# Layer-norm halves of token blocks 3 and 4 finished in their PSUM banks, and the steps around them re-timed

## The chip, the cores and the metric

The kernel runs on one core of one Trainium2 chip. The metric is device time in microseconds (us) of one execution; a comparison uses the median of several runs. TensorE (PE) does the matmuls, VectorE (DVE), ScalarE (ACT) and GpSimd (POOL) do the elementwise work, and SyncE (SP) issues most DMA transfers. Each engine takes its own instructions strictly in program order and waits on semaphores for the others.

## The reference

All arrays are float32. There are 2048 tokens of width 576, 32 query heads and 16 key/value heads of width 128, and a gated MLP of width 4608. Only the last 512 cached keys and values are attended to.

```python
mod = (silu(c) @ w_mod).reshape(1, 6, 1, -1)
sa, ca, ga, sb, cb, gb = mod[:, 0], ..., mod[:, 5]
h = layernorm(x) * (1 + ca) + sa
x = x + ga * attention(h)        # q = h @ wq; softmax(q k^T / sqrt(128)) v; @ wo
h = layernorm(x) * (1 + cb) + sb
x = x + gb * mlp(h)              # ((relu(h @ W_gate)) * (h @ W_up)) @ W_down
```

## The kernel before

**Split operands.** Every float32 matmul operand is held as a rounded part ("hi", type fp32r) and the remainder ("lo"), and a product is made of three matmuls: hi·hi, lo·hi and hi·lo. So each tensor that feeds PE costs one rounding copy and one subtraction.

**Blocks and units.** The tokens are four blocks of 512 (`qb` 0 to 3; the title's blocks 3 and 4 are `qb` 2 and 3). The attention is 128 units, one for each head and block. Units 0 and 1 are block 0 for heads 0 and 1, units 2 and 3 are block 1, units 4 and 5 block 2, units 6 and 7 block 3. While unit `u` computes its scores and its softmax, the same stretch of the program projects the query of unit `u+1`, multiplies probabilities and values of unit `u-1`, and makes pieces of the output projection (`wo`) of older units. So block 2 must be normalised before the projection that stands in unit 3 (`qps` of unit 4), and block 3 before the one in unit 5.

**Order.** The main loop calls the parts of a unit in a fixed order. Between them stand hooks `run(u, k)`, k from 0 to 9, which emit all "steps" whose time is at most `10*u + k`. A step is a piece of side work with a number written by hand: `step("a2.tr0", 29, ...)` is emitted in unit 2 at hook 9. The order of the calls is the order on each engine's queue; SP's DMA issues follow it too, each waiting until its buffer is free.

**Layer norm.** `norm_steps` makes the steps for a block: `stats` (DVE: mean and variance of four tiles of 128 tokens), `rstd` (POOL), `norm` (ACT: `xna`), then for the column groups (0,1), (2,3) and (4): `trans` (PE transposes `xna` into a PSUM bank `lta`) and `affine`. `affine` multiplies by the modulation column and adds the other (`lfa`, an SBUF tile, from `lta` in PSUM), rounds `lfa` to the hi part (`hTa_0` to `hTa_3` and `hTa_8`), and subtracts that from `lfa` to get the lo part (`hTa_4` to `hTa_7`, and the upper half of `hTa_8`). A string such as "aav" says which engine does each of the three passes (a: ACT, v: DVE, p: POOL). `trans` takes its bank from one of three PSUM pools, named "s", "w" and "m" in the table of steps: "s" (two buffers, also the scores), "w" (one, also the `wo` pieces and the gate row `mps`) and "mm" (two, also `qps`, `qm` and `pv`).

**Maxima.** The softmax maxima of a unit are spread over partitions by a small PE matmul (`qm`, in PSUM). `max_bc` reduces them to `r`. In the first four units and the last one (`by_pe`) `r` is split into parts (`rh`, `rr`), transposed on DVE (`mb`), copied by ACT (`mr`), and PE subtracts it from the scores by matmuls with `minus`; in the other units DVE subtracts.

**Gate row and first output weights.** `m2.0` to `m2.4` sum up five pieces of the modulation's third row on DVE (`wmb`), `ga` spreads it by PE (`mps`) and ACT (`mrow`), and the first two output weights are loaded (`wo0.l`, `wo1.l`; tile `roga`), multiplied by it on DVE (`.g`), and split by ACT and POOL (`.c`; tile `woga`).

A `wo` piece is added to the residual by DVE (`acc`), or, where no other user of the "w" bank stands between two pieces, ACT copies the residual into the bank first and the sum back after it ("seeded").

## Time and profile before

| | |
|---|---|
| time, three runs | 2917.99 us median (2914.55 to 2919.14) |
| profiled execution | 2925.96 us, its span 2923.5 us |
| PE busy | 2858.1 us, 98% of the span |
| DVE, POOL, ACT busy | 2161.4 (74%), 2117.4 (72%), 1489.4 (51%) us |
| mean granted TensorE clock | 0.993 |

A row of a timeline gives start, duration, engine, source line, operation, output and inputs with buffer numbers left out, how many instructions are merged into it, and in brackets the idle time before it and what ended that. A row of a table by windows gives the stretch and its length, the busy time of each engine with the number of instructions, and then the granted clock, the DMA engines' share and GB/s. A row of waits gives who waited for whom, the total, how often, and the longest.

### The profile page before, as it was taken

Reading aid. Unit: us, or ns where it says so; the run is one execution under the profiler, and the core shown is the slowest. Engines: PE = TensorE matmul, PEld = TensorE weight load, DVE = VectorE, ACT = ScalarE, POOL = GpSimd, SP = SyncE. Lnnn points to the kernel's source line nnn. Section 1 sums busy time; section 2 is a strip of 40 time slices with the busy share of each in tenths; the row PEclk is TensorE's granted clock in tenths of the full one; section 3 lists DMA queues with packets and bytes.
Section 4 is the critical chain, followed back from the end, with each engine's and each line's share of the span. In section 5 each row is a group of like instructions: output and inputs, shape, how many; then the busy total and the mean of one; then the engine's idle time right before and its main releaser. Section 6 shows DMA issues by size and latency. Waiting matters only on the chain. (4 is left out here: it accounts for less than half of the span.)

```text
span 2923.5 us, 41266 instructions
## 1 busy us (share of the span) xinstructions
PE 2858.1 (98%) x15214; PEld 2490.0 (85%) x15214; DVE 2161.4 (74%) x2981; ACT 1489.4 (51%) x2095; POOL 2117.4 (72%) x1564
## 2 busy tenths in 40 slices
PE   6799999999999999999999999999999999999999
PEld 4588888888888888888888888888888888888888
DVE  7888888888888888777889755666676466666666
ACT  4466666666676666666656444444444122222221
POOL 4588888888889889876778666777787356656553
PEclk9899999999999999999999999999999999999999
DMA  4011222222223223322144456666666944444443
GB/s 151 22 45 53 85 91 80 71 101 90 89 89 108 84 69 118 116 70 86 65 129 144 142 210 220 226 230 224 224 222 251 340 160 152 151 152 153 157 151 104
DMA packets 162697, 396.43 MB, mean 136 GB/s; under 512 B 14912, under 2 KB 61760, under 8 KB 162496
## 3 DMA queue, kind: packets, MB, share of 16 engines
q1 hardware_dynamic: 131472, 282.15, 30.2%
q10 hardware_dynamic: 31024, 111.65, 9.7%
q8 instruction: 120, 1.97, 0.3%
q14 instruction: 81, 0.66, 0.1%
HBM read 268.73 MB, written 153.32 MB: 144 GB/s over the span
## 5 line engine op out<-in xcount | busy, mean ns | idle before, releaser
L539 POOL TENSOR_TENSOR lo<-p,hi 128x1024 fp32r<-128x1024 f32 x256 | 610.0, 2405 | 1.1 <-ACT hi L519 1.1
L548 POOL TENSOR_TENSOR ks<-ks,p 128x512 f32<-128x512 f32 x256 | 344.0, 1344 | 271.8 <-ACT p L532 208.7
L460 DVE TRANSPOSE_TENSOR_REDUCE t<-s 128x32 f32<-128x1024 f32 x256 | 316.8, 1244 | 136.4 <-PE s L457 125.0
L943 PE MATMUL gu<-hop_B,wop 128*128 128x512 f32 (+1 forms) x1512 | 379.0, 394 | 0.9 <-DMA wop<-wk_P 0.9
L943 PEld LDWEIGHTS gu<-hop_B,wop 128*128 128x128 f32 (+1 forms) x1512 | 276.3, 188 | 53.6 <-issue 1.3
L383 PE MATMUL qps<-hTa,wA 128*128 128x512 f32 x1288 | 312.4, 394 | 9.7 <-ACT lfa L365 7.7
L943 PE MATMUL gu<-hop_T,wop 128*128 128x512 f32 (+1 forms) x1260 | 319.9, 393 | 0.0
L599 PE MATMUL wo<-woga,ohi 128*128 128x288 f32 x1472 | 305.9, 301 | 1.5 <-DVE lfa L363 1.5
L383 PEld LDWEIGHTS qps<-hTa,wA 128*128 128x128 f32 x1288 | 244.7, 190 | 62.1 <-ACT lfa L365 8.2
L530 DVE TENSOR_TENSOR p<-s,mb 128x1024 f32<-128x1024 f32 x246 | 290.3, 1219 | 4.1
L519 ACT CAST hi<-p 128x1024 fp32r<-128x1024 f32 x256 | 269.1, 1051 | 7.1
L599 PE MATMUL md<-wogb,hhi 128*128 128x288 f32 x1280 | 263.4, 298 | 5.8 <-DVE acc L610 4.9
L532 ACT ACTIVATE p<-p 128x1024 f32<-128x1024 f32 x246 | 259.9, 1056 | 8.0 <-DVE p L530 7.9
L943 PEld LDWEIGHTS gu<-hop_T,wop 128*128 128x128 f32 (+1 forms) x1260 | 228.4, 188 | 41.0
L610 DVE TENSOR_TENSOR acc<-md,acc 128x576 f32<-128x576 f32 x160 | 120.9, 756 | 177.5 <-PE md L599 177.1
L435 ACT ACTIVATE qhi<-qps 128x512 fp32r<-128x512 f32 x128 | 76.5, 598 | 341.1 <-PE qps L383 341.1
L599 PEld LDWEIGHTS wo<-woga,ohi 128*128 128x128 f32 x1472 | 238.7, 188 | 9.1 <-issue 1.9
L599 PEld LDWEIGHTS md<-wogb,hhi 128*128 128x128 f32 x1280 | 214.9, 190 | 19.1 <-DVE acc L610 6.3
L1054 DVE TENSOR_TENSOR acc<-st_P,acc 128x576 f32<-128x576 f32 x160 | 121.1, 757 | 133.7 <-PE st_P L1045 133.7
L599 PE MATMUL wo<-woga,olo 128*128 128x288 f32 x736 | 216.9, 295 | 0.3 <-POOL olo L588 0.2
L599 PE MATMUL md<-wogb,hlo 128*128 128x288 f32 x640 | 190.1, 297 | 0.0
L588 POOL TENSOR_TENSOR olo<-rb,ohi 128x512 fp32r<-128x512 f32 x128 | 167.3, 1307 | 23.6 <-ACT ohi L584 23.1
(269 smaller groups left out, 7106.6 us busy)
## 6 DMA issues: line engine op xcount, KB each, us to landing
wop<-wk_P SPq DMA_DIRECT2D x133, 640.0 KB
wk_P<-wop ACTq DMA_DIRECT2D x119, 640.0 KB
wr<-wlay SPq DMA_DIRECT2D x68, 384.0 KB
rogb<-wd SPq DMA_DIRECT2D x68, 288.0 KB
againq<-akq SPq DMA_DIRECT2D x18, 640.0 KB
rwA<-wq SPq DMA_DIRECT2D x32, 320.0 KB
wlay<-wg SPq DMA_DIRECT2D x36, 256.0 KB
roga<-wo SPq DMA_DIRECT2D x32, 288.0 KB
```

What stands on the lines that cost most here:

```text
L383: return [lambda i=i, a=a, b=b: nc.tensor.matmul(ps, a, b, start=(i == 0), stop=(i == n - 1)) for i, (a, b) in enumerate(ops)]
L460: nc.vector.tensor_reduce(t4[u][:, 2 * h:2 * h + 2, :].rearrange("p k b -> p (k b)"), t.rearrange("p k (b j) -> p (k b) j", j=32), axis=AX ...
L519: nc.scalar.copy(hi_[u, h], pt[u, h])
L530: nc.vector.tensor_tensor(p, t, bc[u][:, None, :].to_broadcast([P, 2, 512]), op=ALU.subtract)
L532: nc.scalar.activation(p, p, AF.Exp, bias=0.0, scale=1.0)
L539: nc.gpsimd.tensor_sub(lo_[u, h], pt[u, h], hi_[u, h].bitcast(F32))
L548: nc.gpsimd.tensor_tensor(ks_[u], ks_[u], p[:, j, :], op=ALU.add)
L588: nc.gpsimd.tensor_sub(olo[u], o.pop(u), ohi[u].bitcast(F32))
L599: nc.tensor.matmul(ps[:, half, :H2], a[:, sl], w[b][:, cs], start=(n == 0 and seed is None), stop=(n == 5), skip_group_check=seed is not None)
L610: nc.vector.tensor_tensor(av, ps[:, :, :H2], av, op=ALU.add)
L943: nc.tensor.matmul(ps, a, c, start=s not in heir(m) and i == 0 and s not in seeds_of(m), stop=i == len(ops) - 1, skip_group_check=True)
L1054: nc.vector.tensor_tensor(t, ps[:, :, :H2], t, op=ALU.add)
```

## The change

1. For blocks 2 and 3 `affine` makes no `lfa`. It writes the hi part straight from the PSUM bank, then writes the full result back into the same bank, and a new step (`.lo`) lets DVE subtract the hi part from the bank. Engines by group: block 2 "aav", "vvv", "aav"; block 3 "aav" three times.
2. The group (0,1) is transposed after the scores of units 3 and 5 (steps 30.5 and 50.5 and a new hook `run(u, .5)`) instead of ahead of them, group (2,3) of block 3 in the "s" pool one hook earlier, and group (4) of it in "mm". The projections of units 4 and 6 take the groups in the order (2,3), (4), (0,1), with the lo parts of 1 and 0 last.
3. In the `by_pe` units `r` lies in the bank of `qm`, and the two parts are made from it there; `rh` and one copy are gone.
4. `m2.2` moves from step 14 to 5, `m2.3` from 14 to 16, the gate row from 19 to 21, the two weights' loads from 19 and 24 to 10 and 11, their multiplications from 20 and 26 to 23, their splits from 24 and 30 to 29 and 32. `rstd` of block 2 moves from 16 to 14, its fourth `xna` tile to another pool, two of block 3's `stats` from 30 to 33.

```diff
@@ LayerNorm.affine
             add, mul = mods[self.key]
+            if qb > 1:
+                out = {d: (h[8], h[8][64:]) if d == 4 else (h[d], h[4 + d]) for d in ds}
+                for n in range(2):
+                    for d, e in zip(ds, engs):
+                        a, m = add[:, d:d + 1], mul[:, d:d + 1]
+                        dst = self.ps[d] if n else out[d][0]
+                        if e[n] == "v":
+                            nc.vector.tensor_scalar(dst, self.ps[d], m, a, op0=ALU.mult, op1=ALU.add)
+                        else:
+                            nc.scalar.activation(dst, self.ps[d], AF.Identity, bias=a, scale=m)
+                def rest():
+                    for d in reversed(ds):
+                        p0 = 64 if d == 4 else 0
+                        nc.vector.tensor_sub(out[d][1], self.ps[d][p0:], out[d][0].bitcast(F32)[p0:])
+                self.rest[ds] = rest
+                return
@@ proj_ops (late: u in (4, 6))
+        if late:
+            his((2, 3)); both(); los((2, 3)); his((0, 1)); los((1, 0))
...
@@ max_bc
-        r = sp.tile([P, 16], F32, tag="r", name=f"r{u}", bufs=1)
+        r = bps[u][:, 256:272] if by_pe(u) else sp.tile([P, 16], F32, tag="r", name=f"r{u}", bufs=1)
...
-            nc.vector.tensor_copy(rh, r)
-            nc.vector.tensor_copy(rr[:, :, 0], rh.bitcast(F32))
-            nc.vector.tensor_sub(rr[:, :, 1], r, rh.bitcast(F32))
+            nc.vector.tensor_copy(rr[:, :, 0], r)
+            nc.vector.tensor_sub(rr[:, :, 1], r, rr[:, :, 0].bitcast(F32))
@@ norm_steps
+            if key == "a" and qb > 1:
+                step(f"{nm}.lo{k}", t_af[k] + (1 if t_af[k] == 45 else 0), lambda ds=ds: ln.rest[ds]())
@@ the table of steps
-    norm_steps("a2", 2, "a", "wC", "raw", (8, 9, 14, 14), 16, (19,) * 4, (29, 26, 29),
-               (29, 26, 29), (("w", "aav", "vvv"), ("w", "vvv", "vvv"), ("m", "aav")))
+    norm_steps("a2", 2, "a", "wC", "wC", (8, 9, 14, 14), 14, (19,) * 4, (30.5, 26, 29),
+               (30.5, 26, 29), (("w", "aav", "aav"), ("w", "vvv", "vvv"), ("m", "aav")))
...
@@ main loop
         s_half(u, 1)
+        run(u, .5)
         max_pre(u)
```

DVE's queue from the end of unit 2 to the scores of unit 3, before (`lfa` is the affine result, `hTa` the hi and lo parts, `rb` the finished output of a unit, `roga` the second output weight):

```order
L363 TENSOR_SCALAR lfa_2_981<-lta_2_968,mcol_454,mcol_499 128x512
L363 TENSOR_SCALAR lfa_3_983<-lta_2_968,mcol_454,mcol_499 128x512
L367 CAST hTa_2_977<-lfa_2_981 128x512
L367 CAST hTa_3_979<-lfa_3_983 128x512
L371 TENSOR_TENSOR hTa_6_978<-lfa_2_981,hTa_2_977 128x512
L371 TENSOR_TENSOR hTa_7_980<-lfa_3_983,hTa_3_979 128x512
L222 TENSOR_TENSOR roga_941<-roga_941,mrow_860 128x576
L580 TENSOR_TENSOR rb_960<-pv_943,rb_960 128x512
L363 TENSOR_SCALAR lfa_1_1018<-lta_0_1003,mcol_454,mcol_499 128x512
L367 CAST hTa_1_1014<-lfa_1_1018 128x512
L371 TENSOR_TENSOR hTa_5_1015<-lfa_1_1018,hTa_1_1014 128x512
L371 TENSOR_TENSOR hTa_4_1013<-lfa_0_1016,hTa_0_1012 128x512
```

The same queue now, from the same place on:

```order
L359 TENSOR_SCALAR hTa_2_966<-lta_2_957,mcol_454,mcol_499 128x512
L359 TENSOR_SCALAR hTa_3_968<-lta_2_957,mcol_454,mcol_499 128x512
L359 TENSOR_SCALAR lta_2_957<-lta_2_957,mcol_454,mcol_499 128x512 x2
L366 TENSOR_TENSOR hTa_7_969<-lta_2_957,hTa_3_968 128x512
L366 TENSOR_TENSOR hTa_6_967<-lta_2_957,hTa_2_966 128x512
L613 TENSOR_TENSOR rb_949<-pv_932,rb_949 128x512
L366 TENSOR_TENSOR hTa_8_994<-lta_4_0_989,hTa_8_994 64x512
L495 TENSOR_REDUCE t_3_1008<-s_0_1001 128x32
L495 TENSOR_REDUCE t_3_1008<-s_1_1010 128x32
L366 TENSOR_TENSOR hTa_5_1030<-lta_0_1018,hTa_1_1029 128x512
L366 TENSOR_TENSOR hTa_4_1028<-lta_0_1018,hTa_0_1027 128x512
```

Each subtraction now has one operand in PSUM, the rounding copies are gone, and the parts of group (0,1) stand behind the score maxima of unit 3 instead of ahead of them.

DVE's queue behind the spread of unit 2's maxima, before (`r` to `rr` are the maxima and their parts):

```order
L498 TENSOR_REDUCE r_923<-qm_903 128x16
L488 RECIPROCAL ri_925<-qm_903 128x16
L505 CAST rh_928<-r_923 128x16
L506 COPY rr_929<-rh_928 128x16
L507 TENSOR_TENSOR rr_929<-r_923,rh_928 128x16
L508 STREAM_TRANSPOSE mb_927<-rr_929 128x512
L493 STREAM_TRANSPOSE rb_960<-ri_925 128x512
L439 SCALAR_TENSOR_TENSOR qlo_962<-qps_907,qhi_936 128x512
```

And now:

```order
L533 TENSOR_REDUCE qm_892<-qm_892 128x16
L523 RECIPROCAL ri_919<-qm_892 128x16
L539 CAST rr_922<-qm_892 128x16
L540 TENSOR_TENSOR rr_922<-qm_892,rr_922 128x16
L541 STREAM_TRANSPOSE mb_921<-rr_922 128x512
L222 TENSOR_TENSOR roga_751<-roga_751,mrow_896 128x576
L222 TENSOR_TENSOR roga_775<-roga_775,mrow_896 128x576
L528 STREAM_TRANSPOSE rb_949<-ri_919 128x512
L474 SCALAR_TENSOR_TENSOR qlo_951<-qps_902,qhi_928 128x512
```

The maxima stay in the bank `qm`, one copy is gone, and both multiplications of output weights by the gate row stand between the transposed maxima and `qlo`, the low part of unit 3's query.

PE's queue at the projection of unit 4 (in unit 3), before; `wA` is the query weight:

```order
L383 MATMUL qps_1068<-hTa_0_1012,wA_471 128x512 x2
L383 MATMUL qps_1068<-hTa_1_1014,wA_471 128x512 x2
L383 MATMUL qps_1068<-hTa_2_977,wA_471 128x512 x2
L383 MATMUL qps_1068<-hTa_3_979,wA_471 128x512 x2
L383 MATMUL qps_1068<-hTa_8_1029,wA_471 128x512 x2
L383 MATMUL qps_1068<-hTa_4_1013,wA_471 128x512
L383 MATMUL qps_1068<-hTa_5_1015,wA_471 128x512
L383 MATMUL qps_1068<-hTa_6_978,wA_471 128x512
L383 MATMUL qps_1068<-hTa_7_980,wA_471 128x512
```

And now:

```order
L418 MATMUL qps_1042<-hTa_2_966,wA_471 128x512 x2
L418 MATMUL qps_1042<-hTa_3_968,wA_471 128x512 x2
L418 MATMUL qps_1042<-hTa_8_994,wA_471 128x512 x2
L418 MATMUL qps_1042<-hTa_6_967,wA_471 128x512
L418 MATMUL qps_1042<-hTa_7_969,wA_471 128x512
L418 MATMUL qps_1042<-hTa_0_1027,wA_471 128x512 x2
L418 MATMUL qps_1042<-hTa_1_1029,wA_471 128x512 x2
L418 MATMUL qps_1042<-hTa_5_1030,wA_471 128x512
L418 MATMUL qps_1042<-hTa_4_1028,wA_471 128x512
```

The eight matmuls that need groups (2,3) and (4) come first; the eight transposes of group (0,1) now stand just ahead of this list, behind the twelve score matmuls of unit 3.

More of the change, by code (lines that the diff above doesn't have):

```diff
@@ L268, in __init__ @@
             self.qb, self.key, self.where = qb, key, where
-            self.xn, self.ps, self.ready, self.n, self.xt = {}, {}, 0, 0, None
+            self.xn, self.ps, self.rest, self.ready, self.n, self.xt = {}, {}, {}, 0, 0, None
         def stats(self, i):
@@ L371, in affine, with proj_ops, his, los @@
                 eng.tensor_sub(out[d][1], fs[d][p0:], out[d][0].bitcast(F32)[p0:])
-    def proj_ops(ps, w, h):
+    def proj_ops(ps, w, h, late=False):
         ops = []
-        for t in range(4):
-            ops.append((w[:, t, :], h[t]))
-            ops.append((w[:, 5 + t, :], h[t]))
-        ops.append((w[:, 4, :], h[8]))
-        ops.append((w[:, 9, :], h[8]))
-        for t in range(4):
-            ops.append((w[:, t, :], h[4 + t]))
+        def his(ts):
+            for t in ts:
+                ops.append((w[:, t, :], h[t]))
+                ops.append((w[:, 5 + t, :], h[t]))
+        def los(ts):
+            for t in ts:
+                ops.append((w[:, t, :], h[4 + t]))
+        def both():
+            ops.append((w[:, 4, :], h[8]))
+            ops.append((w[:, 9, :], h[8]))
+        if late:
+            his((2, 3))
+            both()
+            los((2, 3))
+            his((0, 1))
+            los((1, 0))
+        else:
+            his(range(4))
+            both()
+            los(range(4))
         n = len(ops)
@@ L1296 @@
     for t in range(5):
[L1297 to L1299 removed]
+        step(f"m2.{t}", (4, 4, 5, 16, 16)[t], lambda t=t: mod_step(2, t, big[2, t]))
+    w_use.add(21)
+    step("ga", 21, setd(mods, "ga", lambda: gate_row(2)))
     sss = (("s", "aap", "vvv"), ("s", "aap", "vvv"), ("s", "aav"))
     www = (("w", "aap", "vvp"), ("w", "aap", "vvp"), ("w", "aap"))
[L1302 to L1305 removed]
+    norm_steps("a2", 2, "a", "wC", "wC", (8, 9, 14, 14), 14, (19,) * 4, (30.5, 26, 29),
+               (30.5, 26, 29), (("w", "aav", "aav"), ("w", "vvv", "vvv"), ("m", "aav")))
+    norm_steps("a3", 3, "a", "wC", "raw", (33, 33, 34, 34), 34, (36,) * 4, (50.5, 45, 49),
+               (50.5, 45, 49), (("w", "aav", "aav"), ("s", "aav", "aav"), ("m", "aav")))
     H = 10 * UNITS.index((HKV - 1, 1, HQ - 1))
@@ L1313 @@
     po = prep_out(wos, 0, wo, "ga")
-    step("wo0.l", 19, po[0])
-    step("wo0.g", 20, po[1])
-    step("wo0.c", 24, po[2])
+    step("wo0.l", 10, po[0])
+    step("wo0.g", 23, po[1])
+    step("wo0.c", 29, po[2])
     po = prep_out(wos, 1, wo, "ga")
-    step("wo1.l", 24, po[0])
-    step("wo1.g", 26, po[1])
-    step("wo1.c", 30, po[2])
+    step("wo1.l", 11, po[0])
+    step("wo1.g", 23, po[1])
+    step("wo1.c", 32, po[2])
     def sk(t, key, d, k):
```

12 lines of the change are left out of this document (3 added, 9 removed).

## The prediction

> **What bounds the kernel now.** I read the page's busy shares first (PE 98%), then the engines' times in two stretches, then PE's waits, then the timelines around the longest of them.
>
> ```profile
> 44.00:146.54 102.54, 74.89 (x322) 59.68 (x323) 85.75 (x137) 49.10 (x68) 53.18 (x37) 0.85 0.07 20
> 150.00:500.00 350.00, 350.00 (x1861) 305.38 (x1860) 285.59 (x424) 238.03 (x319) 290.94 (x175) 1.00 0.22 71
> ```
>
> The second figure of a row is its length, the third PE's busy time. From 150 to 500 us PE never idles: the attention is bound by PE, and whatever shifts its queue ahead of 150 us shifts everything behind. The change's instructions stand almost all in units 0 to 5 (44 to 146.54 us), where PE idles 27.65 us of 102.54 and is granted 0.85 of its clock. So the most there is to win is those waits and the slow clock. They are (waits of PE over the whole program):
>
> ```profile
> PE qps L383 <- ACT lfa L365: 7.7, 1, 7.7
> PE lta L323 <- DVE rb L580: 5.6, 1, 5.6
> PE s L526 <- ACT mr L511: 6.2, 4, 3.0
> PE mps L150 <- DVE wmb L129: 2.9, 1, 2.9
> PE wo L599 <- DVE lfa L363: 1.5, 1, 1.5
> ```
>
> The longest is the projection of unit 4 waiting for block 2's norm. There DVE does this, with POOL beside it:
>
> ```profile
> 81.76 1.52 DVE L363 TENSOR_SCALAR lfa<-lta,mcol,mcol 128x512 f32<-128x512 f32 x2
> 82.80 2.70 POOL L548 TENSOR_TENSOR ks<-ks,p 128x512 f32<-128x512 f32 x2 [1.51 <-ACT p L528]
> 83.20 2.58 DVE L367 CAST hTa<-lfa 128x512 fp32r<-128x512 f32 x2
> 85.45 5.32 POOL L539 TENSOR_TENSOR lo<-p,hi 128x1024 fp32r<-128x1024 f32 x2
> 85.70 5.63 DVE L371 TENSOR_TENSOR hTa<-lfa,hTa 128x512 fp32r<-128x512 f32 x2
> 93.81 1.29 DVE L371 TENSOR_TENSOR hTa<-lfa,hTa 128x512 fp32r<-128x512 f32 x2
> 94.60 0.78 ACT L365 ACTIVATE lfa<-lta,mcol,mcol 128x512 f32<-128x512 f32 x1 [4.50 <-DVE hTa L371]
> ```
>
> Two subtractions take 1.29 us with POOL idle and 5.63 us beside POOL. Whether that goes with the operands' place is told by all instances (minimum, median, maximum, ns):
>
> ```profile
> L371 DVE TENSOR_TENSOR hTa<-lfa,hTa x13: 684/691/2878, 28.6 to 136.0; 128x512 fp32r<-128x512 f32 x10, 64x512 fp32r<-64x512 f32 x3
> L505 DVE CAST rh<-r x5: 127/931/1298, 44.8 to 1630.8; 128x16 fp32r<-128x16 f32 x5
> L507 DVE TENSOR_TENSOR rr<-r,rh x5: 169/169/1266, 45.8 to 1632.2; 128x16 f32<-128x16 f32 x5
> L222 DVE TENSOR_TENSOR roga<-roga,mrow x32: 744/750/2368, 69.4 to 1181.5; 128x576 f32<-128x576 f32 x32
> L580 DVE TENSOR_TENSOR rb<-pv,rb x128: 636/680/693, 66.3 to 1657.4; 128x512 f32<-128x512 f32 x128
> L439 DVE SCALAR_TENSOR_TENSOR qlo<-qps,qhi x128: 650/653/692, 35.5 to 1622.1; 128x512 fp32r<-128x512 f32 x128
> ```
>
> The first four read SBUF alone and stretch to several times their least. The last two have one operand in PSUM, and of 256 none passes 0.693 us. The new subtractions (L366, L540) are of the second kind. The Trainium skill ("SBUF — State Buffer", Who interferes with whom) says why: GpSimd shares a port pair with VectorE, held for a whole instruction, and two SBUF inputs or a two-port mode need it. These rows agree.
>
> **The sum.** PE's queue, at the points I count between (brackets: idle before):
>
> ```profile
> 66.46 2.20 PE L150 MATMUL mps<-wmb,ones 128*128 128x288 f32 x4 [2.88 <-DVE wmb L129]
> 68.04 1.04 PE L455 MATMUL s<-qhi,kv 128*128 128x512 f32 x1
> 71.94 3.35 PE L383 MATMUL qps<-hTa,wA 128*128 128x512 f32 x14
> 83.42 1.50 PE L323 MATMUL lta<-ident,xna 128*128 128x128 f32 x12 [1.20 <-DVE lfa L363]
> 84.68 0.47 PE L455 MATMUL s<-qhi,kv 128*128 128x512 f32 x1
> 95.43 5.92 PE L383 MATMUL qps<-hTa,wA 128*128 128x512 f32 x14 [7.75 <-ACT lfa L365]
> 102.42 0.45 PE L483 MATMUL qm<-t,quad 128*128 128x80 f32 x2 [1.07 <-DVE t L475]
> 110.35 0.39 PE L455 MATMUL s<-qhi,kv 128*128 128x512 f32 x1
> 113.10 3.34 PE L383 MATMUL qps<-hTa,wA 128*128 128x512 f32 x14
> 131.25 1.97 PE L323 MATMUL lta<-ident,xna 128*128 128x128 f32 x8 [5.59 <-DVE rb L580]
> 132.87 0.78 PE L455 MATMUL s<-qhi,kv 128*128 128x512 f32 x1
> 140.30 0.45 PE L483 MATMUL qm<-t,quad 128*128 128x80 f32 x2 [0.32 <-DVE t L475]
> 146.54 0.39 PE L455 MATMUL s<-qhi,kv 128*128 128x512 f32 x1
> ```
>
> At full clock 12 score matmuls take 2.75 us (110.35 to 113.10), so 0.23 each; 12 transposes 1.26 (83.42 to 84.68), so 0.84 for 8.
>
> *Maxima, units 0 to 2.* PE waits for `mr` behind `r`. The stalls of one CAST in unit 0 (0.931−0.127 = 0.8) and of a CAST and a subtraction in units 1 and 2 (up to 1.266−0.169 = 1.1 each) go: −3.0. A PSUM result may cost each step 0.1 more; the dropped copy pays that. The bank of `qm` is freed later, and `pv` takes it next; but behind half of `pv` PE waits for `mr` anyway, so nothing.
>
> *Gate row.* The 2.88 us wait goes, because the row is spread behind unit 2's scores; its matmuls and those scores ran slowly (66.46 to 68.04, 68.04 to 71.94 against 2.75), so 0.8 and 1.15 more: −4.8. The multiplications it feeds read SBUF alone and now stand, both, ahead of `qlo` of unit 3, while POOL works: 2×0.75 plus a stall; of that PE sees about +0.5. Earlier weight loads and the later split cost nothing: `woga` is first read by a `wo` piece in unit 3. The cover is half a unit; without it that piece waits. `rstd` on POOL passes ahead of `ks`, which waits for the second exponential anyway. On SP the two loads now pass three layout copies (`wlay`), which nothing reads before the MLP, and wait only for buffers that are free in unit 0; on POOL the weights' low parts stand behind unit 2's `lo`, ahead of nothing that PE is near.
>
> *Unit 2's end.* The wait of 1.20 goes and 8 transposes move behind the scores: −2.0.
>
> *Unit 3 to its spread (84.68 to 102.42: 17.7 us).* Two more rows carry this stretch and unit 5's:
>
> ```profile
> 101.22 0.27 DVE L468 TENSOR_REDUCE qm<-t 128x16 f32<-128x64 f32 x1
> 118.92 1.06 ACT L532 ACTIVATE p<-p 128x1024 f32<-128x1024 f32 x1
> ```
>
> Counted from the first score matmul: `qlo` is ready just ahead, at −0.3. DVE goes on with `ks` (some 0.7), two passes that write hi and two that write the bank (0.76 each, from 81.76) and two subtractions (1.29), and ends at 4.6. PE is done with the scores at 2.75; its next work, eight transposes, needs the "w" bank that DVE still reads: it waits 1.85, transposes (0.84), ends at 5.4. Then eight matmuls run to 7.3 without a wait, four more for `hTa_0` and `hTa_1`. ACT meanwhile makes two hi passes and two into the bank (0.78 the last, 0.72 apart: 3.0), so DVE subtracts from 8.5 to 9.8, PE's last two matmuls wait for that some 1.4 in all, and DVE's `t` (101.22 to 102.42: 1.2) ends at 11.0. In all 11.0 for 17.7: −6.7. The 7.75 us wait and the half clock of the 5.92 us projection are in that.
>
> *Spread to unit 4's scores (102.42 to 110.35: 7.9 us).* The same PE work stands here, and the maxima of unit 3 had no stall to lose. Before, a slow stretch of 3.4 us lay in it; I expect one again, since PE has just worked little (the clock, below). Two more tiles' statistics stand between `mb` and `qlo`, whose third score matmul waits a little: +0.5. Without a slow stretch it is 1.0 less: −0.5.
>
> *Unit 4 (110.35 to 132.87).* The waits of 1.5 and 5.59 go, and eight half-speed transposes (131.25 to 132.87) move behind the scores: −8.7. ACT takes over DVE's add of one `wo` piece, hidden by the next PE work.
>
> *Unit 5 (132.87 to 140.30: 7.4 us).* Here part of it is paid back. Ahead of unit 5's scores PE has 5.6 us of work behind the second `wo` piece (12 `pv` at 0.23, 12 `wo` of 288 columns at 0.13, 12 transposes at 0.105), and ACT in that time two copies (0.63), the first exponential and its rounding (1.06 each), some 3.7 with the hand-overs: so its four passes of group (2,3) start 1.9 before the scores and end 1.1 after they began. The second exponential, which stood there, queues behind them; its readers on POOL are not needed before the next unit. DVE's two subtractions free the score bank at 2.5, where PE, six matmuls in (1.4), has waited 1.1. Scores end at 3.9, transposes at 4.7. ACT comes to `hTa_8` behind the second exponential, its rounding and a copy (2.7) and makes two passes (1.5): done at 5.3, subtracted at 6.0, and PE waits 0.3. A weight's copy (0.7) and four passes (3.0) later, at 9.0, DVE subtracts to 10.2, and `t` ends at 11.4. In all 11.4 for 7.4: +4.0.
>
> *To 146.54.* Same work, but behind a low stretch: +1.5 for a slow window.
>
> Sum: −3.0 −4.8 +0.5 −2.0 −6.7 +0.5 −8.7 +4.0 +1.5 = −18.7. A matmul's end, 0.39 behind its start where the next one follows after 0.23, is counted as work but stood ahead of each lost wait as well: 0.16, some eight times, −1.3. Together −20.
>
> **Unknown price.** No row shows a pass that reads and writes PSUM. Below stands a copy into PSUM, above a read and a write one after the other:
>
> ```profile
> 114.38 0.63 ACT L632 COPY wo<-acc 128x576 f32<-128x576 f32 x1
> ```
>
> So 0.63 to 0.78+0.63 = 1.4 us. I take 0.78, the row of the same operation from PSUM. Nine such passes stand on the chains of units 3 and 5 (two of DVE, seven of ACT): at 1.4 they add 9×0.62 = 5.6 us, at 0.63 they save 1.4.
>
> **The clock.** Stretches of 3.41 us:
>
> ```profile
> 76.82:80.23 3.41, 2.28 (x12) 1.00 0.00 0
> 80.23:83.64 3.41, 2.21 (x14) 1.00 0.31 89
> ...
> 100.72:104.13 3.41, 1.77 (x8) 1.00 0.00 0
> 104.13:107.54 3.41, 3.41 (x10) 0.50 0.00 0
> ```
>
> With 2.28 and 2.21 us of PE work in a stretch the clock stayed; with 1.77, and no idle time over 1.07 in it, the next stretch was slow, which costs up to 1.7 us. Behind both new spreads PE works about 0.8 of 3.9 us, so I count one slow stretch at each. The Trainium skill ("TensorE: Matmul & The Clock Gate", Why this matters for your kernels) warns only of idle gaps above some 3 us between bursts. By that neither place would slow down and the sum would be the first rival's; the 1.77 row speaks against it.
>
> **Rivals.**
> - *No slow stretch.* For it: the longest new wait is 1.85 us, and before the clock mostly fell behind waits of 2.9 us and more. Then the +1.5 goes and the +0.5 becomes −0.5: −22.5, 2895.5. Against: the 1.77 row. Chance 0.13.
> - *Less, by new waits.* In-place passes at 1.4 (+5.6) and two more slow windows (+3.4): −11, 2907. Nearly the same if the subtractions wait for POOL after all, so that the change doesn't do what it says: four that PE waits for, by 2.878−0.684 = 2.2 each, +8.8. Against that: 256 instances. Chance 0.18.
> - *No change.* The front's gain is given back to a DMA later. Against: 350 us of unbroken PE work. Chance 0.07.
> - *Slower.* The many gaps of 0.3 to 1.9 us keep PE at half clock from unit 2 to 5, some 50 us of work at full clock. Each slow stretch costs 1.7 us, so 12 more eat the 20 us; at 50 us of doubled work it would be +30, 2948. Before, with longer gaps, a full stretch always brought the clock back. Chance 0.05.
>
> **The numbers.** Forecast: −20 against the profiled execution's 2925.96 us, and as well against the median, 2917.99, 0.3% lower: 2898. Chance of −14 to −22: 0.57. The range, 2893 to 2909, takes in the first rival's gain (2895.5, and 1.4 more with cheap passes) and the second's loss with 2 us on top; it leaves out the last two rivals (0.12) and the tails of the others. A change of 0.2% (5.8 us) is about what the runs can tell. Faster 0.88, same 0.07, slower 0.05.
>
> **What would show it.** L366 within 0.70 us each, all ten. PE's waits for `lfa`, `rb` and `wmb` gone; new ones for L366 (at the "w" bank 1.9, the score bank 1.2, the last lo parts 1 to 2 twice). Unit 6's scores near 126 us. Clock 0.5 for some 3.4 us behind the spreads of units 3 and 5. I am wrong if L366 stretches beside POOL, if in-place passes exceed 1.4 us, or if the later stages lose what units 1 to 4 won.

## The result, and the profile after

The changed kernel takes 2898.20 us (median of six runs, 2893.46 to 2904.06) against 2918.57 for the kernel before on the same chip (six runs, 2914.55 to 2922.90): a ratio of 0.9932, 95% interval 0.9921 to 0.9942. That is 20.4 us less; the forecast was 2898. Its profiled execution took 2898.73 us, with a span of 2895.9.

First the same stretch by windows as before the change, now from 44 us to the first score matmul of unit 6, and the attention behind it:

```profile
44.00:125.94 81.94, 72.19 (x320) 57.46 (x321) 66.81 (x119) 56.08 (x78) 51.61 (x36) 0.90 0.07 22
150.00:500.00 350.00, 348.48 (x1848) 303.62 (x1848) 286.69 (x424) 235.98 (x317) 291.31 (x174) 1.00 0.22 74
```

Unit 6 starts at 125.94 us instead of 146.54, so the stretch is 20.6 us shorter. Not all of that is the change: unit 0's scores began at 37.05 us in the profiled execution of before and at 35.06 in this one, and in the traces of the experiments below they begin anywhere from 34.2 to 36.9. From unit 0's scores to unit 6's it is 18.6 us. PE's idle time in the stretch fell from 27.65 to 9.75 us, and the granted clock rose from 0.85 to 0.90. Behind it PE is as full as it was: the 1.52 us missing from 350 are one wait, which before stood at 505.70 us, just behind that window.

The rest of the program, from unit 6's scores to the end, is another 7.0 us shorter in these two executions. Of that, 1.1 us are the change: the last unit of the attention makes its maxima in the new way too (x2, below). The other 5.9 lie behind the attention. From unit 6's scores to the end it is 2777.0 us in the kernel before and 2775.9 in x5, which has only the in-place passes, against 2767.7 to 2771.1 in the eleven other kernels, so this may belong to the change too; why is not shown. In the medians, which differ by 20.4, there is little room for it: the profiled execution of before was 7.4 us above its own median.

PE's waits in that stretch of the changed kernel (who waited for whom, total, how often, longest):

```profile
PE pv L605 <- DVE rr L540: 2.8, 3, 0.9
PE s L559 <- ACT mr L544: 2.1, 1, 2.1
PE qps L418 <- DVE hTa L366: 2.1, 4, 0.7
PE lta L323 <- DVE hTa L366: 1.8, 1, 1.8
PE qm L518 <- DVE t L510: 1.1, 2, 0.6
PE s L490 <- DVE hTa L366: 0.8, 1, 0.8
```

The waits of 7.7 for `lfa`, 5.6 for `rb` and 2.9 for `wmb` are gone. New are those for the subtractions, L366: at the "w" bank 1.8, at the score bank 0.8, at the last low parts 0.7 at most. The maxima now hold the bank of `qm` for longer: `pv` waits 2.8 us for it in this stretch, 1.7 before, while the wait for `mr` fell from 5.2 to 2.1. The passes and subtractions themselves (minimum, median, maximum, ns), and one pair of subtractions beside POOL:

```profile
L366 DVE TENSOR_TENSOR hTa<-lta,hTa x10: 680/692/695, 76.6 to 116.4; 128x512 fp32r<-128x512 f32 x8, 64x512 fp32r<-64x512 f32 x2
L361 ACT ACTIVATE lta<-lta,mcol,mcol x8: 738/751/752, 75.0 to 115.0; 128x512 f32<-128x512 f32 x8
76.55 1.29 DVE L366 TENSOR_TENSOR hTa<-lta,hTa 128x512 fp32r<-128x512 f32 x2
76.15 4.68 POOL L572 TENSOR_TENSOR lo<-p,hi 128x1024 fp32r<-128x1024 f32 x2
```

All ten subtractions lie within 0.70 us, though several stand beside POOL, and a pass from a bank into the same bank takes 0.75 us on ACT (0.82 on DVE). PE's queue at the points that the forecast counted between:

```profile
47.05 0.79 PE L490 MATMUL s<-qhi,kv 128*128 128x512 f32 x1 [0.32 <-ACT p L561]
59.77 0.39 PE L490 MATMUL s<-qhi,kv 128*128 128x512 f32 x1
73.24 0.47 PE L490 MATMUL s<-qhi,kv 128*128 128x512 f32 x1
77.99 1.06 PE L323 MATMUL lta<-ident,xna 128*128 128x128 f32 x8 [1.76 <-DVE hTa L366]
84.53 0.58 PE L518 MATMUL qm<-t,quad 128*128 128x80 f32 x2 [0.56 <-DVE t L510]
93.93 0.39 PE L490 MATMUL s<-qhi,kv 128*128 128x512 f32 x1
107.28 0.48 PE L490 MATMUL s<-qhi,kv 128*128 128x512 f32 x1
109.71 0.47 PE L490 MATMUL s<-qhi,kv 128*128 128x512 f32 x1 [0.79 <-DVE hTa L366]
118.15 0.45 PE L518 MATMUL qm<-t,quad 128*128 128x80 f32 x2 [0.55 <-DVE t L510]
125.94 0.39 PE L490 MATMUL s<-qhi,kv 128*128 128x512 f32 x1
```

And the clock around the two spreads, in stretches of 3.41 us (PE's busy time is the third figure, the granted clock the third from the end):

```profile
81.22:84.63 3.41, 2.11 (x8) 0.98 (x6) 2.67 (x6) 1.44 (x3) 2.41 (x2) 1.00 0.00 0
84.63:88.04 3.41, 2.46 (x7) 1.90 (x8) 2.71 (x10) 1.34 (x3) 0.00 (x0) 0.51 0.30 96
88.04:91.46 3.42, 3.42 (x10) 2.65 (x9) 3.25 (x11) 1.80 (x3) 1.66 (x3) 0.50 0.00 0
115.35:118.77 3.42, 2.23 (x10) 1.18 (x9) 2.44 (x6) 0.97 (x2) 2.77 (x2) 1.00 0.00 0
118.77:122.18 3.41, 3.41 (x15) 3.21 (x14) 2.96 (x6) 1.81 (x3) 1.16 (x1) 0.51 0.40 118
```

Slow stretches came behind both spreads, two of them at unit 3's.

### The profile page after: what moved, and what is told of

It reads as the page before. It is cut to its first block, busy times and chain, and to the rows that moved or that the text cites. A ratio compares the mean times of both kernels' runs of the same rounds, so it can differ in the third digit from the quotient of the medians.

```text
span 2895.9 us, 41262 instructions
## 1 busy us (share of the span) xinstructions
PE 2852.8 (99%) x15214; PEld 2485.6 (86%) x15214; DVE 2145.8 (74%) x2967; ACT 1496.0 (52%) x2105; POOL 2115.4 (73%) x1564
## 4 chain that ended last, share of the span: by engine, by line
PE 91%; POOL 3%; DVE 3%; ACT 2%; issue 1%; DMA 1%; SPq 0%; ACTq 0%; POOLq 0%; DVEq 0%
PE gu L976 26%; PE wo L632 13%; PE qps L418 13%; PE md L632 8%; PE st_P L1078 6%; PE s L491 4%; PE s L490 4%; PE s L492 4%; PE pv L607 4%; PE pv L606 4%; PE pv L605 4%; PE qm L518 1%; POOL lo L572 1%; ACT p L565 0%; DVE ws L783 0%
## 5 line engine op out<-in xcount | busy, mean ns | idle before, releaser
L641 ACT COPY acc<-wo 128x576 f32<-128x576 f32 x233 | 148.2, 636 | 66.8 <-PE wo L632 61.6
```

The costliest lines, as they stand in the source:

```text
L641: nc.scalar.copy(av, ps[:, :, :H2])
```

## The experiments

Each run was timed beside the kernel before. Where times differ by a few us, the place is read from the profiled execution. That is one execution, and it lay anywhere from 6.4 us below its kernel's median (x2) to 7.4 above (before), so places and medians need not agree. The table gives the time between the first score matmul of a unit (s) and the spread of its maxima (q), and in the last column how much of s1 to s6 was granted half the clock.

| | median us | s1-s2 | s2-s3 | s3-q3 | q3-s4 | s4-s5 | s5-q5 | q5-s6 | s1-s6 | at half clock |
|---|---|---|---|---|---|---|---|---|---|---|
| before | 2918.57 | 18.19 | 16.64 | 17.74 | 7.93 | 22.52 | 7.43 | 6.24 | 96.69 | 27.0 |
| changed | 2898.20 | 12.72 | 13.47 | 11.29 | 9.40 | 13.35 | 10.87 | 7.79 | 78.89 | 13.8 |
| x1 | 2904.05 | 12.91 | 13.50 | 15.54 | 6.65 | 14.00 | 12.85 | 7.81 | 83.26 | 14.1 |
| x2 | 2904.53 | 13.56 | 15.90 | 10.03 | 7.92 | 13.34 | 10.88 | 6.25 | 77.88 | 6.9 |
| x3 | 2900.52 | 16.98 | 13.24 | 12.26 | 6.65 | 13.99 | 10.89 | 6.24 | 80.25 | 7.8 |
| x4 | 2895.41 | 12.00 | 13.50 | 11.69 | 6.66 | 13.96 | 10.90 | 6.24 | 74.95 | 5.4 |
| x5 | 2914.36 | 17.45 | 20.61 | 10.69 | 9.10 | 21.47 | 6.90 | 6.22 | 92.44 | 24.7 |
| d1 | 2892.13 | 13.08 | 13.47 | 11.29 | 6.75 | 14.01 | 10.88 | 6.23 | 75.71 | 4.3 |
| v2 | 2902.99 | 11.94 | 13.50 | 11.25 | 8.31 | 17.33 | 10.93 | 7.78 | 81.04 | 12.1 |
| best1 | 2898.62 | 11.73 | 13.49 | 11.00 | 6.73 | 18.11 | 11.52 | 6.25 | 78.83 | 8.0 |
| e1 | 2900.25 | 12.83 | 13.49 | 11.28 | 6.75 | 13.99 | 12.53 | 6.22 | 77.09 | 3.8 |
| best2 | 2892.70 | 11.75 | 13.49 | 11.69 | 6.65 | 14.00 | 10.87 | 6.24 | 74.69 | 3.4 |
| best3 | 2891.13 | 11.75 | 13.49 | 10.99 | 6.74 | 14.02 | 10.58 | 6.23 | 73.80 | 0 |

**x1: the second pass writes SBUF.**

```
+                t = pp.tile([P, 1024], F32, tag="p", ...)      # groups (0,1) and (2,3)
+                fs = {d: t[:, 512 * j:512 * j + 512] for j, d in enumerate(ds)}
-                        dst = self.ps[d] if n else out[d][0]
+                        dst = fs[d] if n else out[d][0]
-  nc.vector.tensor_sub(out[d][1], self.ps[d][p0:], ...)
+  nc.vector.tensor_sub(out[d][1], fs[d][p0:], ...)
```

> The changed kernel, but for column groups (0,1) and (2,3) of blocks 2 and 3 the second pass writes an SBUF tile instead of the bank, and the subtraction reads that tile; places, engines and the number of instructions stay. My theory (a DVE instruction with two SBUF inputs is held while POOL works, one with a PSUM operand is not): the pairs of subtractions that stand beside POOL's work stretch from 1.29 us to between 2.5 and 5.6 us, as two of them did before (5.63). Beside POOL stand the pair at 76.55 us, the one at 82.14 and the one at 115.75; the one at 108.28 has POOL idle. The wait of the transposes behind the first pair goes (1.76, the bank is free a pair of subtractions earlier), but the projection of unit 4 waits for it instead. Estimate +2 to +4 for unit 3 and +1 to +2 for unit 5: +3 to +6 us against the changed kernel (2901 to 2904), most of the eight L366 with SBUF operands over 0.9 us. Rival (the new places of the steps make the gain, not the operand's place): all stay within 0.70 us each and the time is that of the changed kernel or up to 2.6 us less, since the banks come free earlier.

Measured: 2904.05 us, ratio to before 0.995 (0.9938 to 0.9962), 5.9 above the changed kernel. DVE's subtractions (L371) and POOL's work beside them:

```profile
76.46 5.52 DVE L371 TENSOR_TENSOR hTa<-lfx,hTa 128x512 fp32r<-128x512 f32 x2
85.75 1.29 DVE L371 TENSOR_TENSOR hTa<-lfx,hTa 128x512 fp32r<-128x512 f32 x2
117.66 3.75 DVE L371 TENSOR_TENSOR hTa<-lfx,hTa 128x512 fp32r<-128x512 f32 x2 [0.22 <-ACT lfx L366]
76.32 5.11 POOL L577 TENSOR_TENSOR lo<-p,hi 128x1024 fp32r<-128x1024 f32 x2
114.19 4.72 POOL L577 TENSOR_TENSOR lo<-p,hi 128x1024 fp32r<-128x1024 f32 x2
118.87 1.98 POOL L182 TENSOR_TENSOR wA<-rwA,wA 128x640 fp32r<-128x640 f32 x1
```

PE's wait for them:

```profile
PE qps L423 <- DVE hTa L371: 9.5, 4, 5.7
```

The first pair starts 0.14 us behind POOL's `lo` instructions and lasts 5.52 us; in the bank the same pair took 1.29. The pair at 117.66 stretches to 3.75. The pair that I had expected to stretch in unit 3's middle had been pushed, by the first one, to where POOL was idle, and took 1.29. PE waits 5.7 us for the first. Unit 3 to its spread is 4.25 longer, but two slow stretches, from 81.61 to 88.43 us, lie in it here and behind the spread in the changed kernel: to unit 4's scores it is 1.5 longer. Unit 5 is 2.0 longer. Only four of the eight subtractions stretched, not most of them. With nothing but the operand's place altered, the time moved as the theory said, and the rival is out. The run says a second thing: with the operand in SBUF, some 15 of the 20 us are still won, by the rest of the change.

**x2: the maxima's parts as before** (r in SBUF, `rh`, one copy more):

```
-        r = bps[u][:, 256:272] if by_pe(u) else sp.tile(...)
+        r = sp.tile([P, 16], F32, tag="r", name=f"r{u}", bufs=1)
+            nc.vector.tensor_copy(rh, r)
+            nc.vector.tensor_copy(rr[:, :, 0], rh.bitcast(F32))
```

> The changed kernel with the maxima's parts made as before: r in SBUF, rounded to rh, copied, subtracted (three instructions). My theory: the stalls of unit 0 (0.8) and units 1 and 2 (up to 1.1 each) come back: +3.0 us (2 to 4), as periods of units 0 to 2 that are longer by 0.8 to 1.1 each, and one of unit 3 if POOL works there. Rival (PE waits for mr no longer, since other waits end last now): within 1 us of the changed kernel.

Measured: 2904.53 us, ratio 0.9949 (0.9936 to 0.9961). Behind the spread of unit 2, DVE, POOL and PE:

```profile
69.49 1.65 DVE L540 CAST rh<-r 128x16 fp32r<-128x16 f32 x1
71.17 1.19 DVE L541 COPY rr<-rh 128x16 f32<-128x16 f32 x1
66.36 4.75 POOL L574 TENSOR_TENSOR lo<-p,hi 128x1024 fp32r<-128x1024 f32 x2
71.04 1.29 POOL L623 TENSOR_TENSOR olo<-rb,ohi 128x512 fp32r<-128x512 f32 x1
73.89 1.21 PE L561 MATMUL s<-mr,minus 128*128 128x512 f32 x4 [2.54 <-ACT mr L546]
```

And in the last unit of the attention:

```profile
1609.98 1.30 DVE L540 CAST rh<-r 128x16 fp32r<-128x16 f32 x1
1613.01 1.20 PE L561 MATMUL s<-mr,minus 128*128 128x512 f32 x4 [0.98 <-ACT mr L546]
```

Behind unit 2's spread a CAST of 16 columns ends when POOL's `lo` ends (71.14 and 71.11), and the copy behind it when POOL's `olo` ends (72.36 and 72.33). Units 0 and 1 lose 0.8 each, as expected. Unit 2 loses 2.4, more than the 1.1 expected, and unit 3 gives 1.26 of it back, since DVE's passes over block 2 are then further along when its scores begin (PE waits 0.5 us at the "w" bank instead of 1.8). The sum of these places, 2.8, is the theory's. But the last unit is one of the `by_pe` units too, and neither the forecast nor this expectation counted it: there the CAST takes 1.30 us, against 0.11 in the changed kernel, and from that unit's scores to this place x2 is 1.14 us longer. So the maxima are worth some 4.0 us by places. The median moved by 6.3, yet s1 to s6 in the profiled execution is 1.0 *shorter* than the changed kernel's: it had 6.9 us less at half clock. The executions of x2 reach from 2898.1 to 2909.0. How many slow stretches there are differs between executions by as much as this part is worth.

**x3: gate row, weights and rstd at the old steps.**

```
-    step(f"m2.{t}", (4, 4, 5, 16, 16)[t], ...)  ->  (4, 4, 14, 14, 16)[t]
-    step("ga", 21, ...)                         ->  19
     wo0.l/.g/.c  10, 23, 29 -> 19, 20, 24       wo1.l/.g/.c  11, 23, 32 -> 24, 26, 30
     a2: "wC", "wC", rs 14   -> "wC", "raw", rs 16
```

> The changed kernel with the steps of the gate row, of its modulation pieces, of rstd of block 2 and of the first two output weights as before (gate row at 19, loads at 19 and 24, multiplications at 20 and 26, splits at 24 and 30; the fourth xna tile in its old pool). My theory: the wait of PE for wmb (2.9 us) and the slow clock behind it come back, +4.8 us, less nothing for the multiplications, which PE did not wait for: +4 to +5 us, all of it between the scores of unit 1 and those of unit 3. Rival (the wait is filled with something else, or the multiplications of the weights, which have two SBUF inputs, now stall DVE where the new chain needs it): 0 to +2, or above +7 if a weight is late for its first output piece.

Measured: 2900.52 us, ratio 0.994 (0.9928 to 0.9952). PE's wait is back:

```profile
PE mps L150 <- DVE wmb L129: 2.8, 1, 2.8
```

Unit 1 is 4.26 us longer and unit 2 0.23 shorter, between unit 1's scores and unit 3's as the theory had it, +4.0. Unit 3 to its spread is 0.97 longer, which I had not expected. The trace says why:

```profile
81.58 2.14 DVE L222 TENSOR_TENSOR roga<-roga,mrow 128x576 f32<-128x576 f32 x1
80.74 5.20 POOL L572 TENSOR_TENSOR lo<-p,hi 128x1024 fp32r<-128x1024 f32 x2
```

At its old step the second weight's multiplication, which has two SBUF inputs, stands beside POOL's `lo` and takes 2.14 us instead of 0.75. It stands ahead of group (4)'s subtraction, the projection of unit 4 waits 2.22 us for that (0.17 in the changed kernel), and a slow stretch, from 86.04 to 89.45 us, falls on the projection. So the rival, that the multiplications stall DVE in the new chain, holds as well as the theory. That the median moved by only 2.3 is the clock again: this trace lost no stretch in unit 5, and one less in unit 3.

**x4: the projections of units 4 and 6 in the old order** (`late` always false):

```
-            qst[u] = ps, proj_ops(ps, wqs[h], hT[qb], u in (4, 6))
+            qst[u] = ps, proj_ops(ps, wqs[h], hT[qb])
```

> The changed kernel with the projections of units 4 and 6 in the old order of column groups, (0,1) first and the low parts last. My theory: the end of the stretch is set by DVE (t behind the last subtractions), not by these matmuls: the first eight no longer run while ACT makes the hi parts of group (0,1), but four low-part matmuls instead of two behind the last subtraction end about when t does: 0 to +1 us. Rival (PE's filled time was worth its length): eight matmuls of 0.23 are no longer covered, +1.8 in unit 3 and in unit 5, +3.7 us.

Measured: 2895.41 us, ratio 0.992 (0.9907 to 0.9932): not slower. In unit 3 the projection now starts late, in one piece, and 3.4 of its 5.2 us at half clock:

```profile
80.47 5.22 PE L418 MATMUL qps<-hTa,wA 128*128 128x512 f32 x14 [0.87 <-ACT hTa L361]
85.52 0.34 PE L518 MATMUL qm<-t,quad 128*128 128x80 f32 x2
```

Its end sets the spread 0.4 later than in the changed kernel; in unit 5, at full clock, the difference is 0.03. The new order of column groups is worth next to nothing, as expected: DVE's maxima end the stretch.

**x5: the in-place passes alone, in the kernel before.** The new branch of `affine` and the `.lo` steps, all else as before:

```
+            if qb > 1:                                  # affine: the branch of the changed kernel
+            if key == "a" and qb > 1:                   # norm_steps
+                step(f"{nm}.lo{k}", t_af[k] + ..., lambda ds=ds: ln.rest[ds]())
```

> The kernel before with one part of the change alone: blocks 2 and 3 finished in their banks (hi part written, full result written into the bank, subtraction from the bank), at the old steps, by the engines of the old table, maxima and gate row as before. My theory: the subtractions keep 0.65 us each, so the 4.3 us stall ahead of unit 4's projection and smaller ones go; but the bank is held longer (two more passes and the subtractions, about 1.5 to 3 us), and the transposes of group (0,1), which stand ahead of the scores in units 2 and 4, wait for that: -6 us against the kernel before, between -9 and -2. Rival (the operand's place makes nearly all of the gain in units 3 to 5): -14 or more. Second rival (the new places are what makes the gain; the bank held longer eats what the subtractions win): 0 or slower.

Measured: 2914.36 us over 11 runs, against 2917.63 for the kernel before beside it: -3.3, ratio 0.9988 (0.9979 to 0.9997). All ten subtractions took at most 0.695 us. But ahead of unit 3's scores and of the output piece of unit 4:

```profile
83.92 2.79 PE L323 MATMUL lta<-ident,xna 128*128 128x128 f32 x12 [4.22 <-DVE hTa L366]
122.22 0.82 PE L617 MATMUL wo<-woga,ohi 128*128 128x288 f32 x2 [4.51 <-DVE hTa L366]
```

Unit 3 to its spread is 7.05 shorter than before, as short as in the changed kernel, but unit 2 is 3.97 longer: the bank is held by two passes and two subtractions more, and the transposes that stand ahead of the scores wait. Neither rival is right. The operand's place and the new places of the transposes need each other: alone the passes give 3 of the 20 us.

**d1: PE's waits around the two spreads filled.**

```
+    zero = ...                                    # a column of zeros
+    def warm(u, n):
+        for i in range(n):
+            nc.tensor.matmul(qst[u][0], minus, zero[:, :1].to_broadcast([P, 512]), start=False, ...)
     qproj, u in (4, 6):  warm(u, 2) ahead of the last two matmuls, warm(u, 2) behind them
     spread, u == 3:      warm(4, 4) behind it
```

> The changed kernel with 12 matmuls of 512 columns more, which add zeros to the query's bank where PE waits anyway: two ahead of the last two low parts and two behind them in units 3 and 5, four behind the spread of unit 3. They cost 0.23 us each and wait for nothing new. My theory (a stretch of 3.41 us in which PE works too little is followed by one at half clock, whatever the length of the single gaps: in six traces none with over 2.3 us of work was, and each with under 1.45 was): the stretches before both spreads, with 2.11 and 2.22 us of work in the changed kernel's trace, get 0.9 to 1.8 more, and the slow ones at 84.7 to 91.5 and 118.8 to 122.3 us go. The time from unit 3's spread to unit 4's scores falls from 9.4 to about 6.6 us, from unit 5's to unit 6's from 7.8 to 6.3; the median, in which other phases of the stretches are mixed, by 2 to 4 us. Rival (the slow clock follows idle gaps or the waits themselves): both periods and the median stay, or the median rises by up to 1 us, since the added matmuls delay the ones behind.

Measured: 2892.13 us, ratio 0.9918 (0.9904 to 0.9931); three of its four executions lie within 2891.78 and 2892.43, at a mean clock of 0.999. The stretches ahead of both spreads, and those behind:

```profile
83.82:87.23 3.41, 3.00 (x12) 1.72 (x11) 2.31 (x5) 1.09 (x2) 2.04 (x2) 1.00 0.00 0
87.23:90.64 3.41, 3.38 (x15) 2.48 (x15) 3.19 (x11) 1.86 (x4) 0.15 (x1) 1.00 0.38 96
114.54:117.95 3.41, 3.23 (x14) 2.07 (x12) 2.92 (x6) 1.39 (x2) 3.41 (x2) 1.00 0.07 22
117.95:121.36 3.41, 3.29 (x21) 2.81 (x20) 2.83 (x6) 1.39 (x3) 1.10 (x2) 1.00 0.38 104
```

Spread to scores fell from 9.40 to 6.75 and from 7.79 to 6.23, as expected, and the median by 6.1, more than expected (4 by the ratios to the kernel before). Work that computes nothing made the kernel faster: a stretch with little PE work is paid for in the next.

**v2: DVE makes the passes of one column of block 3's group (2,3)**:

```
-    norm_steps("a3", ... (("w", "aav", "aav"), ("s", "aav", "aav"), ("m", "aav")))
+    norm_steps("a3", ... (("w", "aav", "aav"), ("s", "aav", "vvv"), ("m", "aav")))
```

> The changed kernel with one of block 3's columns of group (2,3) passed on DVE (both passes) instead of ACT. My theory (what is paid back in unit 5 is ACT's chain of in-place passes, for which DVE waits 2.9 and 2.0 us): DVE's two passes, 1.6 us, run while ACT makes its two; the subtractions start 1.4 us earlier, and with them the second half of the scores (its 0.8 us of wait goes), the second exponential, group (4) and group (0,1): unit 5 from its scores to its spread falls from 10.9 to 9.5 us, -1.4 us in all. Rival (PE's own work and DVE's maxima set the end of unit 5): 10.9 stays, or rises by up to 1 us since DVE has 1.6 us more to do.

Measured: 2902.99 us, ratio 0.9954 (0.994 to 0.9967): slower than the changed kernel. In unit 4:

```profile
104.38 0.81 DVE L359 TENSOR_SCALAR hTa<-lta,mcol,mcol 128x512 fp32r<-128x512 f32 x1 [3.56 <-ACT hTa L361]
105.23 0.75 ACT L361 ACTIVATE lta<-lta,mcol,mcol 128x512 f32<-128x512 f32 x1 [0.88 <-DVE hTa L359]
106.01 0.82 DVE L359 TENSOR_SCALAR lta<-lta,mcol,mcol 128x512 f32<-128x512 f32 x1 [0.82 <-ACT lta L361]
109.20 0.66 PE L323 MATMUL lta<-ident,xna 128*128 128x128 f32 x4 [3.78 <-DVE qlo L474]
```

The two engines take turns, each pass waiting for the other engine's last: four passes took 3.3 us, no less than on ACT alone (3.0). Both work on halves of one tile (two banks); that this is the reason was not tested. And DVE's stand in its queue ahead of the second subtraction of the maxima and of `qlo`, so that PE waits 3.78 us for unit 5's scores. Unit 5 itself did not get shorter. Both theories missed this, and the edit could not answer its question; e1 did.

**best1: d1, v2 and the passes of a group in the order hi, full, hi, full.**

```
-                for n in range(2):
-                    for d, e in zip(ds, engs):
+                for d, e in zip(ds, engs):
+                    for n in range(2):
-                    for d in reversed(ds):
+                    for d in (ds if engs[0] == "aav" else ds[::-1]):
-            los((1, 0))
+            los((0, 1))
```

> The changed kernel with both of these and, for groups done by ACT alone, the passes in the order hi, full, hi, full instead of hi, hi, full, full, with the subtractions in that order, so that the first of them can start while ACT is at the second column. My theory: -1.4 for the shared group, -0.5 in each of units 3 and 5 for the order, -2 to -4 for the filled stretches: -4.5 to -6.5 us against the changed kernel, 2892 to 2894. Rival (each of these waits is only replaced by the next one): within 2 us of it.

Measured: 2898.62 us, ratio 0.9935 (0.9923 to 0.9948). Unit 4 is 4.1 longer than in d1, by v2's waits, which hid the rest; unit 3 gained 0.29. The edit reorders DVE's group of block 2 as well, not only the groups done by ACT alone.

**e1: d1 with ACT's chain longer.**

```
+                        if qb == 3 and not n and d in (1, 3):
+                            nc.scalar.activation(dst, self.ps[d], AF.Identity, bias=a, scale=m)   # again
```

> The kernel with the filled stretches (d1, 2892.1 us), and two ACT passes more in block 3: the hi part of one column of group (2,3) and of one of group (0,1) is written a second time with the same values, 0.76 us each. My theory (what the change pays back in unit 5 is ACT's chain: its passes, the second exponential, its rounding, the next passes, the last subtraction): unit 5 from its scores to its spread grows by both, from 10.9 to 12.4 us, +1.5 us in all, with DVE's waits for ACT's passes up by as much. Rival (PE's own matmuls and DVE's maxima set the end of unit 5, ACT has time to spare): 10.9 stays.

Measured: 2900.25 us, ratio 0.9932 (0.992 to 0.9945). Unit 5 to its spread: 12.53 for 10.88, +1.65. DVE's wait for ACT's passes in d1:

```profile
DVE hTa L368 <- ACT lta L363: 5.6, 3, 3.1
```

and in e1:

```profile
DVE hTa L371 <- ACT lta L363: 7.2, 3, 3.9
```

So each us on ACT's chain in unit 5 is a us of that stretch, which is the forecast's account of what unit 5 pays back. The median rose by 8.1, more than the 1.65 of the place; its executions had mean clocks of 0.997 and 0.998 where three of d1's four had 0.999. Where the stretches lay in those without a profile was not seen.

**best2 and best3: unit 0 filled too, and the order hi, full, hi, full with it.** best2 adds six zero matmuls in the first projection, three ahead of unit 0's spread and seven behind it; best3 adds best1's order of passes.

```
     qproj, u == 0:  + warm(0, 6) ahead of the last two matmuls
     qproj, u == 1:  + warm(1, 3) behind the last matmul
     spread, u == 0: + warm(1, 7) behind it
```

> The kernel with the filled stretches, with more zero matmuls in unit 0: six ahead of the last two matmuls of the first projection (PE waits 1.7 us there), three ahead of unit 0's spread and seven behind it (it waits 1.1 and 2.1 us). My theory: the stretch with 0.46 us of work at 42.9 us gets 2.3 more, and the two slow stretches from 46.3 to 53.2 us, in which unit 0's subtraction and unit 1's scores run, go; unit 0 from its scores to unit 1's falls from 12.2 to about 11 us, unit 1's from 13.1 to about 12: -2 to -3 us against the 2892.1 of d1, and up to 1 more where a stretch at 33 us was slow. Rival (the waits there leave no room, or the start differs so much between executions that the fills miss): within 1 us.

> The same, with the passes of groups done by ACT alone in the order hi, full, hi, full, and the subtractions and last low parts in that order. My theory: DVE's first subtraction behind the maxima no longer waits for ACT's fourth pass: unit 3 from its scores to its spread 0.3 to 0.5 shorter, unit 5 0.5: -0.8 to -1 us against the kernel without this. Rival (the hi part of the second column is 0.75 us later, and the projection with it): within 0.3, or up to 0.5 longer in each unit.

Measured: best2 2892.70 us, ratio 0.9913 (0.99 to 0.9927); best3 2891.13, ratio 0.9908 (0.9893 to 0.9923). In best2's trace units 0 and 1 ran at full clock: s1 to s2 fell from 13.08 to 11.75, and from unit 0's scores to unit 2's it is 2.0 us less than in d1, as expected. But one stretch in unit 3 was slow (the one before it holds PE's wait at the "w" bank, 1.75 us, which no zero matmuls fill), and the median is d1's: there the expected -2 to -3 did not come. In best3 no stretch between 25 and 150 us was slow; units 3 and 5 are each 0.3 shorter than in d1, where 0.3 to 0.5 and 0.5 were expected. best3 is the fastest kernel here, 27 us below the kernel before and 7 below the changed one; its lead over d1, 1.0, is no more than the executions spread.

## Why the prediction was right

*Operands.* The mechanism held: L366 at most 0.695 us beside POOL, 1.29 for a pair, and 5.52 when the one operand moves to SBUF (x1). The Trainium skill ("SBUF — State Buffer", Who interferes with whom) says the same; x1 is the direct test that the forecast lacked. x1 and x5 bound what it is worth: 5.9 us with the new places and 3.3 without them. The rest of the 20 is re-timing, gate row and maxima.

*Maxima*, -3.0: x2 gives 2.8 in the places that the forecast counted. The sizes per unit were off (0.8, 0.85 and 1.2 net) and cancel. The last unit's 1.14 was left out.

*Gate row*, -4.8: x3 gives +4.3 in unit 1. The +0.5 for the two multiplications was not spent: they stretched to 2.83 us beside POOL, but PE's transposes stood ahead of the scores and covered it.

*Unit 2's end*, -2.0: unit 2 is 3.17 shorter in all, 1.1 of which is the maxima's term.

*Unit 3 to its spread*, 11.0: 11.29, with every wait where it was put: 1.76 for 1.85 at the bank, 0.7 for some 1.4 at the last two matmuls. *Unit 4*, -8.7: -9.17. *Unit 5*, 11.4: 10.87; the score bank was waited for 0.79 instead of 1.1. e1 shows the chain was the right one.

*In-place pass*, taken at 0.78, between 0.63 and 1.4: it took 0.75 on ACT and 0.82 on DVE.

*The clock* is the mis-sized term, and it was right partly by luck. +0.5 from unit 3's spread to the next scores was +1.47, because two slow stretches came, not one. d1 shows that section at 6.75 without any, so two cost 2.65; behind unit 5 one cost 1.56, as forecast (+1.5). But x2, x3 and x4 have no slow stretch behind unit 5 at all, with the same work there. The forecast took as fixed what differs between kernels by where the 3.41 us stretches happen to be cut, and between executions: the changed kernel's six runs reach from 2893.46 us at a mean clock of 0.999 to 2904.06 at 0.995. The rival "no slow stretch", 2895.5, is near what the fastest of the six was. The medians of x2 and e1 moved farther than their places did (6.3 for 4.0 us, and 8.1 for 1.65).

*The total.* The forecast was -20; from unit 0's scores to unit 6's the traces show -18.6. The two clock terms came out 1.0 too small together. The other places gave 0.9 more than their own terms, which is most of the 1.3 counted for the ends of matmuls. The last unit, which the forecast left out, adds -1.1, and so the errors cancel. The mechanisms were right, but that the median fell within 0.2 us of the forecast is luck, since executions of the changed kernel differ by 10.

The other rivals did not happen: no later stage gave the front's gain back, and the many small gaps did not hold PE at half clock.

## What to carry to other kernels

A DVE instruction with two SBUF inputs, and here also a cast or a copy out of SBUF, costs what it waits for on POOL as well; an operand left in PSUM takes that away, but the bank is then held longer, so the next user of the bank has to be moved behind, or most of the gain stays there. Where PE is the bound, count PE's work by stretches of 3.41 us (here the limit lay at 1.3 us of work, by the count below), not by single waits: the cheapest gain here was to fill them with matmuls that compute nothing. Before an edit of 1 to 5 us is judged by a median, see how many slow stretches each trace had.

## What the hardware showed that was not expected

The clock follows the sum of PE's work in a stretch, also without any long gap. In the traces of the two kernels and of x1 to x4, from the first record of the clock (26 to 32 us) up to 150 us, every full-clock stretch in which PE was busy for under 1.45 us was followed by one at half clock, and none with over 2.3 us; between, both occur. The changed kernel's 2.11 and 2.23 us (shown above) were followed by slow ones, while the second row here is at full speed behind 1.50 us, in x2:

```profile
71.98:75.39 3.41, 1.50 (x9) 1.27 (x10) 3.38 (x7) 1.85 (x3) 0.35 (x1) 1.00 0.00 0
75.39:78.80 3.41, 3.41 (x22) 2.89 (x21) 3.31 (x6) 3.35 (x5) 1.03 (x1) 1.00 0.00 0
```

That band is mostly a matter of counting. The profile ends a matmul of 512 columns 0.39 us after its start, while the next one starts after 0.23 where nothing holds it, so each matmul with a wait behind it counts 0.16 us too much. Count instead the time to the next start in a full queue: 0.226 us for 512 columns, 0.130 for 288, 0.105 for a transpose, 0.068 for `qm`. Then the changed kernel's two stretches hold 1.30 and 1.31 us of work, and x2's holds 1.38. In all 13 traces, from the first record of the clock to the last matmuls, there are 10827 full-clock stretches. All 47 with at most 1.31 us of work were followed by a slow one; of the others one was, with 1.33, beside one with 1.32 that was not.

The Trainium skill ("TensorE: Matmul & The Clock Gate", Why this matters for your kernels) speaks of idle gaps above some 3 us; in the changed kernel's stretch from 81.22 to 84.63 no single gap was longer than 0.65 us, and the slow stretch came, so here the measurement decides. By the same count, transposes are work: a stretch of x1, from 112.33 us, with 0.84 us of them and 0.72 of other matmuls was followed by full clock. So are matmuls on zeros: without its 1.13 us of them, the stretch of d1 from 83.88 us would hold 1.01, and it was followed by full clock.
